# Attention ahead of a routed expert layer: the tokens' logits as products of their own, and one table for the order of the steps

## The chip, the core and the metric

The kernel runs on one core of a Trainium2 chip. The core has five engines with a queue each, which work through their instructions in program order and wait for each other through semaphores: TensorE (PE in the profile, with its weight loads as PEld), VectorE (DVE), ScalarE (ACT), GpSimd (POOL) and SyncE (SP), which here issues most of the DMA transfers. The metric is the device time of one execution in microseconds (us), lower is better. All data are 32-bit floats, unless something else is said.

## What is computed

The reference, cut to what matters:

```
B, H, S, Ns, D = 8, 8, 512, 32, 64            # attention
scores = x @ state.T * 0.125;  a = softmax(scores)     # tokens look at the 32 states
xread = a @ state                                      # a row for each token
scores2 = state @ x.T * 0.125; a2 = softmax(scores2)   # states look at the 512 tokens
sread = a2 @ x                                         # a row for each state
rows = concat(xread, sread) -> (8, 544, 512)           # heads side by side: 4352 rows of 512
...
logits = rows @ w_gate                                 # 8 experts
gate = sigmoid(rows @ w_local)
for each batch, for each row s in order:
    e = argmax(logits[s]) if s == 0 or gate[s] < 0.5 else the expert of the row before
    out[s] = softmax(logits[s])[e] * (relu(rows[s] @ w1[e]) @ w2[e])   # 512 -> 1024 -> 512
```

So every one of the 4352 rows goes through one of eight experts, and which one depends on the logits of that row and, through the gate, on the rows before it in its batch.

## The kernel before

The work has three stages, one after the other on TensorE.

**Attention** (classes `Attention` and `Batch`, lines 147 to 509). It goes batch by batch, b = 0 to 7. The eight heads of a batch lie as two groups (u = 0, 1) of four heads, 128 partitions each. For a batch:
- `scores` (L377): TensorE makes the scores of 128 head-and-state rows over 512 tokens, into two PSUM banks. Both softmaxes start from them.
- The softmax over states: `turned` (L410, VectorE transposes 32x32 blocks so that the 32 states lie along the free dimension), `over_states` (VectorE maximum L417, GpSimd subtraction L418), `exponents` (L422, ScalarE), `shares` (VectorE sum L426, L427, reciprocal L428, GpSimd product L429), `turn_back` (L435, VectorE transposes into the tile `a`).
- The softmax over tokens: `maximum` and `scaled` (L387, L391), `exponents_over_tokens` (L399, ScalarE, which also sums), `turn` (L445, transposes on TensorE), `turned_to` (L448, ScalarE copies them out), `state_reads` (L458, TensorE), `states_to` (L464, ScalarE), `states_to_rows` (L470 a transpose, L473 four DMAs to the tensor `rows` in DRAM).
- `token_reads` (L482): for each of four chunks c of 128 tokens, two products of `a` with the block-diagonal matrix `sd`. `sd` holds 256 state columns for each group and, beside them, the 9 columns of states times gate weights (`gates`, L212, L215), so that one product of 265 columns gives the values and a half of the token's nine logits. The 530 columns are copied to `xr` (L485), by VectorE for chunk 1 and by ScalarE for the others; GpSimd adds the two halves of the logits into `lt` (L507), and the values go to `rows` by one DMA for a batch (L508).
- `state_logits` (L500, L502): the logits of the 32 state rows.

The order of all these steps is written by hand in `run` (lines 224 to 355): three batches `now`, `then`, `later` are in work at once. Scores and transposes have one PSUM bank for each of four names (`s0`, `s1`, `t0`, `t1`), the values two tiles of two banks (`vps`). Every chunk of every batch is read before the stage ends.

**Routing** (class `Routing`). `choose` (L584 to L590) makes maxima and first-best experts from `lt`: once for batches 0 to 6, inside the attention, and once for batch 7 at the start of `route`. `route` then turns them to rows of 544 (`seq`, L611), carries the choice forward with a scan (L618, L620), turns back (`back`, L624), counts the rows of each expert (L637, L638), and works out, in a chain of small VectorE steps, in which slot each row is. `keep(n)` (L600) issues n products with no use for their result, 9 and 5 and 20 and 8 times. The expert of the first pair is known at L691; then SP issues its weights (L913), and after `two` (L763) GpSimd fetches the first 256 rows (L863).

**Experts** (`experts`, from L824). Rows are taken in pairs of blocks, 256 rows of one expert at a time, and nine small tiles. The first product is at L1139; from there TensorE works without a break. Its buffers are in memory that the attention has released.

Of the kernel before, what the change touches and what calls it, by code (L numbers as in the profile page):

```python
# [50 lines left out]
def kernel(  # L51
# [31 lines left out]
    def banks(ctx, n):  # L83
        ps = ctx.enter_context(tc.tile_pool(name="ps", bufs=n, space=PSUM))
        return lambda parts=P, n=512, dt=F32: ps.tile([parts, n], dt, tag="ps", name="ps")

# [6 lines left out]
    lt = keep.tile([P, B, NC, E + 1], F32, name="lt")  # L93

# [5 lines left out]
    with ExitStack() as phase:  # L100
        make_identity(nc, ident)
        start = Attention(phase, tc, xn, xt, st, stt, wgl, wgs, lt, rows)
        route.constants(ident)
        nc.gpsimd.memset(lt, 0.0)
        start.diagonal(range(2))
        nc.gpsimd.memset(none, 0.0)
        nc.sync.dma_start(out=rows[NT:].rearrange("o q x -> o (q x)"), in_=none)
        start.run(route)
    with ExitStack() as phase:
        bank = banks(phase, 6)  # L110

        sums = phase.enter_context(tc.tile_pool(name="sums", bufs=1, space=PSUM))
        sums = [sums.tile([P, 512], F32, name=f"sum{i}") for i in range(2)]
        experts(phase, tc, bank, sums, w1, w2, rows, slots, route, route.route(bank, sums, lt, slots), out)
# [21 lines left out]
A = G * SC * 4  # L136


class Attention:


    def __init__(self, ctx, tc, xn, xt, st, stt, wgl, wgs, lt, rows):
        nc = self.nc = tc.nc
        self.xn, self.xt, self.lt, self.rows = xn, xt, lt, rows
        self.wg, self.wh = wgs[:, 0], wgs[:, 1]
        once = ctx.enter_context(tc.tile_pool(name="once", bufs=1))
        self.xp = ctx.enter_context(tc.tile_pool(name="xp", bufs=3))
        self.wk = ctx.enter_context(tc.tile_pool(name="wk", bufs=2))
        self.tp = ctx.enter_context(tc.tile_pool(name="tp", bufs=2))
        self.sm = ctx.enter_context(tc.tile_pool(name="sm", bufs=4))  # L150
        self.ps = ctx.enter_context(tc.tile_pool(name="aps", bufs=1, space=PSUM))
        self.vps = ctx.enter_context(tc.tile_pool(name="vps", bufs=2, space=PSUM))

# [5 lines left out]
        self.x_t = {0: self.load_t(0)}  # L159
# [4 lines left out]
        self.x_t[1] = self.load_t(1)  # L164
        self.x_n = {0: self.load_n(0)}


        self.sd = once.tile([P, B, G * VW], F32, name="sd")
        nc.gpsimd.memset(self.sd, 0.0)
# [7 lines left out]
    def diagonal(self, ks):  # L177
        nc = self.nc
        for k in ks:
            r = slice(32 * k, 32 * k + 32)  # L180
            to = self.sd[r, :, E + 1:E + 1 + D].rearrange("p b (g d) -> p b g d", g=G)
            nc.scalar.copy(to[:, :, :, DH * k:DH * k + DH],
                           self.states_of[r].rearrange("p (b g d) -> p b g d", b=B, g=G))

    def load_t(self, b):
        nc = self.nc
        xs = []
        for i in range(2):
            x_t = self.xp.tile([P, KT // 2, S], F32, name=f"x_t{i}")
            nc.sync.dma_start(out=x_t.rearrange("p k s -> p (k s)"), in_=self.xt[b][:, i * D * 2:(i + 1) * D * 2])  # L190
            xs.append(x_t)
        return xs

    def load_n(self, b):
        x_n = self.xp.tile([P, SC, G, KT, DH], F32, name="x_n")
        self.nc.sync.dma_start(out=x_n.rearrange("p c u k d -> p (c u k d)"), in_=self.xn[b])
        return x_n
# [4 lines left out]
    def bank(self, name, parts=P):  # L202
        return self.ps.tile([parts, 512], F32, name=name)

    def gates(self):
        nc = self.nc
        ws = [self.bank(f"t{u}") for u in range(G)]
        for u, w in enumerate(ws):
            r = slice(64 * u, 64 * u + 64)
            for b in range(B):  # L210
                for k in range(KT):
                    nc.tensor.matmul(w[32 * k:32 * k + 32, b * (E + 1):(b + 1) * (E + 1)],  # L212
                                     lhsT=self.states(b)[r, k, :], rhs=self.wh[r, k, :], start=True, stop=True)
        for u, w in enumerate(ws):
            nc.scalar.copy(self.sd[:, :, u * (E + 1 + D):u * D + (u + 1) * (E + 1)],  # L215
                           w[:, :B * (E + 1)].rearrange("p (b e) -> p b e", b=B))

    def keep(self, n):

        for i in range(n):  # L220
            self.nc.tensor.matmul(self.idle[:, 0, :], lhsT=self.zero[:, :P], rhs=self.zero, start=True, stop=True)

    def run(self, route):

        self.ident = route.ident
        self.idle = self.vps.tile([P, G, 512], F32, name="v")
        self.keep(10)
        now, then = Batch(self, 0), Batch(self, 1)
        now.scores()
        for b in (2, 3):  # L230
            self.x_t[b], self.x_n[b - 1] = self.load_t(b), self.load_n(b - 1)

        for u in range(G):
            now.turned(u)
            now.over_states(u)
        now.maximum(0)
        now.scaled(0)
        now.exponents(0)
        self.gates()
        now.exponents(1)  # L240
        now.exponents_over_tokens(0)
        now.shares(0)
        now.maximum(1)
        now.scaled(1, self.nc.vector)
        now.exponents_over_tokens(1)
        now.shares(1)
        self.keep(6)
        now.turn(0)
        self.diagonal([2, 3])
        then.scores()  # L250
        now.turn(1)
        now.turn_back(0)
        now.turn_back(1)
        for u in range(G):
            then.turned(u)
            then.over_states(u)
        now.token_reads(0)
        now.turned_to(0)
        now.turned_to(1)
        now.state_reads()  # L260

        later = Batch(self, 2)
        self.load(0)
        then.maxima()
        then.exponents(0)
        then.exponents(1)
        then.exponents_over_tokens(0)
        then.shares(0)
        then.exponents_over_tokens(1)
        then.shares(1)  # L270
        now.invert()
        now.token_reads(1)
        now.states_to()
        now.token_reads(2)
        now.states_to_rows()
        later.scores()
        then.invert()
        later.maxima()
        then.turn(0)
        then.turned_to(0)  # L280
        then.turn(1)
        now.token_reads(3)
        then.turned_to(1)
        then.turn_back()
        later.exponents_over_tokens(0)
        later.turned(1)
        later.exponents_over_tokens(1)
        later.turned(0)
        later.over_states()
        now.logits()  # L290
        later.invert()
        then.token_reads(0)

        for b in range(1, B):
            now, then, later = then, later, Batch(self, b + 2) if b + 2 < B else None
            if later:
                later.scores()
            now.state_reads()
            self.load(b)
            if b == B - 2:  # L300
                then.turn(0)
                then.turn(1)
            if 1 < b < B - 1:
                now.turn_back()
            if b == B - 2:
                for u in range(G):
                    then.exponents(u)
                    then.shares(u)
                    if u == 0:
                        now.states_to()  # L310
            elif then:
                then.exponents()
                now.states_to()
                later.maxima()
            else:
                now.states_to()
            if b > 1:
                now.token_reads(0)
            if later:
                then.shares()  # L320
            now.token_reads(1)
            now.states_to_rows()
            if b == B - 2:
                then.turn_back(0)
            if later:
                then.turn(0)
                then.turn(1)
                later.exponents_over_tokens(0)
            if then:
                then.turned_to(0)  # L330
            now.token_reads(2)
            if then:
                then.turned_to(1)
            if b == B - 2:
                then.turn_back(1)
            if later:

                later.turned(1)
                later.exponents_over_tokens(1)
                later.turned(0)  # L340
                for u in range(G) if b == B - 3 else (None,):
                    later.over_states(u)
            if b == B - 1:
                route.choose(self.lt, 0, b)
                now.state_logits()
                now.token_reads(3)
# [923 lines left out]
```

## Time and profile before

| what | value |
|---|---|
| median of three runs | 560.93 us (559.71 to 562.62) |
| profiled execution, its own time | 559.81 us |
| its span, first to last instruction | 558.0 us |
| mean granted TensorE clock | 0.985 |
| TensorE busy over the span | 529.5 us, 95% |
| VectorE busy over the span | 377.8 us, 68% |
| TensorE's last token read of batch 7 ends (L482) | 83.30 us |
| first product of the experts starts (L1139) | 111.75 us |
| TensorE busy from 112 to 260, and from 260 to 400 us | 148.00 of 148, 140.00 of 140 |

How to read it: the span is cut by stage. In a stage, each engine's busy time is set against the stage's length, and then the timeline of one engine shows its instructions in order of start, each with the idle time ahead of it and what ended that idle time. Instructions overlap at their ends, so the time that one of a row of equal instructions costs is the distance from one start to the next, not its own duration. The row in the page that names the chain which ended last covers only the last instructions here, and says nothing of the attention.

### The profile page before, as it was taken

The page shows a single profiled execution, that of the slowest core. Times are in us where ns is not written, and L with a number is a line of the kernel's source. Part 1 is how long each engine was busy: PE and PEld are TensorE (multiplying, and loading weights), DVE is VectorE, ACT ScalarE, POOL GpSimd, SP SyncE. Part 2 cuts the span into 40 slices and gives each one's busy share as a digit, 9 for nine tenths or more (in the row PEclk, how much of TensorE's full clock was granted, in tenths as well). Part 3 has the DMA queues.
Part 4 walks back from the last instruction along what each step waited for, and adds up shares of the span by engine and source line. Part 5 has one row for each costly group of instructions (what it writes and reads, how often), then busy time and mean ns, then how long its engine had stood idle before and what let it go on. Part 6 is the DMA issues. An engine that isn't in the chain of part 4 may idle for free. (4 is left out here: it accounts for less than half of the span.)

```text
span 558.0 us, 12712 instructions
## 1 busy us (share of the span) xinstructions
PE 529.5 (95%) x4800; PEld 457.9 (82%) x4803; DVE 377.8 (68%) x625; ACT 168.1 (30%) x336; POOL 287.1 (51%) x366
## 2 busy tenths in 40 slices
PE   6879985999999999999999999999999999999994
PEld 2556662698989888898989898989899999989993
DVE  5879987673948474747565666665676766667674
ACT  4656651411132213231313122222232322223230
POOL 6444530165555555656464647463764546565454
PEclk9899997899999999999999999999999999999998
DMA  8999742689998989898979897966566575846652
GB/s 308 414 340 363 267 163 79 188 308 418 364 382 321 357 304 359 309 355 308 375 286 380 304 369 292 361 205 229 166 239 226 187 275 150 279 143 246 231 189 102
DMA packets 50793, 155.44 MB, mean 279 GB/s; under 512 B 9169, under 2 KB 9297, under 8 KB 47394
## 3 DMA queue, kind: packets, MB, share of 16 engines
q1 hardware_dynamic: 43202, 135.85, 66.6%
q0 software_dynamic: 7520, 18.69, 9.7%
q8 instruction: 40, 0.66, 0.5%
q14 instruction: 31, 0.25, 0.1%
HBM read 136.68 MB, written 17.89 MB: 277 GB/s over the span
## 5 line engine op out<-in xcount | busy, mean ns | idle before, releaser
L857 POOL DMA_INDIRECT xg<-rows,row x132 | 148.3, 1124 | 30.6 <-issue 30.1
L972 DVE TENSOR_TENSOR a<-a,a 128x1024 f32<-128x1024 f32 x64 | 76.8, 1220 | 21.1 <-DMA a<-in_w_dram 19.7
L1055 PE MATMUL ps<-xt,a 128*128 128x128 f32 x720 | 88.6, 276 | 0.0
L1055 PE MATMUL sum<-xs,a 128*128 128x128 f32 x720 | 87.8, 275 | 0.0
L1055 PEld LDWEIGHTS ps<-xt,a 128*128 128x128 f32 x720 | 84.4, 192 | 2.1 <-issue 1.8
L1055 PEld LDWEIGHTS sum<-xs,a 128*128 128x128 f32 x720 | 84.0, 192 | 0.0
L972 DVE TENSOR_TENSOR c<-c,c 128x1024 f32<-128x1024 f32 x64 | 75.4, 1219 | 3.0 <-DMA c<-in_w_dram 2.5
L1095 PE MATMUL ps<-c,h 128*128 128x256 f32 x312 | 74.7, 382 | 0.0
L1095 PEld LDWEIGHTS ps<-c,h 128*128 128x128 f32 x312 | 58.0, 190 | 10.9 <-issue 3.7
L1095 PE MATMUL ps<-c,hs 128*128 128x256 f32 x256 | 60.5, 379 | 0.0
L1038 POOL DMA_INDIRECT out_dram<-y,tok x32 | 34.5, 1079 | 43.6 <-DVE c L972 27.1
L1095 PEld LDWEIGHTS ps<-c,hs 128*128 128x128 f32 x256 | 48.6, 190 | 6.6
L1095 PE MATMUL sum<-c,h 128*128 128x256 f32 x200 | 47.2, 379 | 0.0
L972 DVE TENSOR_TENSOR h<-s,s 128x512 f32<-128x512 f32 x15 | 10.4, 692 | 54.2 <-ACT s L1078 54.2
L1095 PEld LDWEIGHTS sum<-c,h 128*128 128x128 f32 x200 | 38.0, 190 | 5.2
L871 POOL COPY tick<-s 1x1 f32<-1x1 f32 x45 | 16.3, 363 | 49.7 <-ACT s L1078 49.5
L482 PE MATMUL v<-sd,a 128*128 128x265 f32 x128 | 34.8, 406 | 4.7 <-DVE a L435 3.3
L1006 ACT COPY sum<-ps 128x256 f32<-128x256 f32 (+1 forms) x31 | 14.3, 460 | 71.0 <-PE ps L1055 49.5
L482 PEld LDWEIGHTS v<-sd,a 128*128 128x128 f32 x128 | 22.8, 193 | 12.0 <-DVE xr L485 3.5
L871 POOL COPY tick<-r 1x1 f32<-1x1 f32 x41 | 12.2, 299 | 36.6 <-ACT r L1100 34.3
L1100 ACT ACTIVATE r<-sum,prob 128x256 f32<-128x256 f32 x32 | 15.2, 475 | 51.7 <-PE sum L1095 49.2
L1095 PE MATMUL sum<-c,hs 128*128 128x256 f32 x128 | 30.2, 379 | 0.0
(228 smaller groups left out, 734.1 us busy)
## 6 DMA issues: line engine op xcount, KB each, us to landing
c<-in_w_dram SPq DMA_DIRECT2D x68, 512.0 KB, 7.8
a<-in_w_dram SPq DMA_DIRECT2D x64, 512.0 KB, 8.2
at<-in_w_dram SPq DMA_DIRECT2D x18, 1024.0 KB, 9.1
ct<-in_w_dram SPq DMA_DIRECT2D x18, 1024.0 KB, 7.8
x_t<-in_xt_dram SPq DMA_DIRECT2D x16, 512.0 KB, 7.9
x_n<-in_xn_dram SPq DMA_DIRECT2D x8, 1024.0 KB, 10.9
rows<-xr SPq DMA_DIRECT2D x8, 1024.0 KB, 4.2
xg<-rows,row POOLq DMA_INDIRECT x132, 5.2
```

The costliest lines, as they stand in the source:

```text
L482: nc.tensor.matmul(v[:, u, :VW], lhsT=self.a[:, u, c * P:c * P + P], rhs=at.sd[:, b, u * VW:(u + 1) * VW], start=True, stop=True)
L857: nc.gpsimd.indirect_dma_start(out=to.rearrange("p k t -> p (k t)"), out_offset=None, in_=rows.rearrange("n q x -> (n q) x"), in_offset=ba ...
L871: nc.gpsimd.tensor_copy(tick, value)
L972: nc.vector.tensor_tensor(out, a, b, op=op)
L1006: nc.scalar.copy(y, x)
L1038: nc.gpsimd.indirect_dma_start(out=out, out_offset=to, in_=y, in_offset=None, bounds_check=NT - 1, oob_is_err=False)
L1055: nc.tensor.matmul(to[:, m * P:m * P + P], lhsT=w[:, j, m * P:m * P + P], rhs=x[:, j, :], start=begin and m == 0 and j == 0, stop=(m == FK ...
L1095: nc.tensor.matmul(to, lhsT=x[:, m, :], rhs=w[:, m, :], start=begin and m == 0, stop=(m == FK // 2 - 1), skip_group_check=True)
L1100: nc.scalar.activation(to, t, Act.Copy, scale=p)
```

## The change

**The logits.** `sd` keeps only the 256 state columns of each group. The 9 columns of states times gates go to a tile of their own, `gl`, padded with zeros to 32 columns. A new step `logits` makes, for a batch, eight products of 32 by 128 outputs into one bank, over both groups, and `logits_turned` transposes that bank on VectorE into `lt`, which now has 32 columns for each chunk. GpSimd's addition of halves is gone.

**The values.** `token_reads` writes both groups, 512 columns, into one bank; all the copies to `xr` are ScalarE's.

**The order.** `run` and its three batches in work are gone. A string `STEPS` lists every step (two letters, batch, group or chunk), and `more` issues them in that order until a condition ends. Nearly all steps are now for one group (half a batch). The scores have four banks that rotate (`sp`), all else in the attention four banks (`p`); `e1` has five buffers of half a batch, `a` ten, `xr` three. In the table, `ch0` is `choose` for batches 0 to 6. All that stands after `ch1` is issued inside `route`: `reads(2)` and `reads(3)` take the places of `keep(9)` and `keep(5)`, a `reads(1)` follows `back`, and `reads(NB)` issues the rest after the counts. So eight of the 32 chunks (batch 5: one, batch 6: three, batch 7: four) are read inside the routing, with their ScalarE copies and the last three DMAs to `rows`. The third `keep` goes from 20 to 14. `route.more_constants` moves from the end of the attention to its start, and GpSimd's clearing of `gl`, `lt`, `sd` behind the constants.

**The memory.** What the late reads use (`a`, `xr`, `sd`, `lt`, bank pool `p`) is on the other side of memory and is released after the first yield of the routing; the experts' buffers are opened in two parts around this, and the routing has four banks until then, six after it.

The diff, cut to its core:

```
-        start.diagonal(range(2))
-        nc.gpsimd.memset(none, 0.0)
-        nc.sync.dma_start(out=rows[NT:].rearrange("o q x -> o (q x)"), in_=none)
+            start.clear()
+            route.more_constants()
             start.run(route)
...
+STEPS = """
+sc0 xt11 xt10 tr01 ga sd1 tr00 xt21 mx01 sd3 mo00 xt31 gl mo01 sb00 sd0 sc1 mx00 sb01 xn0 ex00 sd2 tr10 nb0 zs00
+et00 tr11 et01 xt20 tu00 mo10 ec00 iv0 tu01 sb10 mx10 xn1 ex01 mx11 ec01 zs01 ex10 nb1 sr0 zi01 et11 zs10 ml01
...
+tb60 vv53 ml71 xr42 tb70 lg6 wr4 xr53 tb71 vv60 lt6 ch0 lg7 xr60 vv51 vv52 lt7 xr51 ch1 vv73 xr52 vv70 xr73 vv50
+xr70 vv61 xr50 vv72 wr5 xr61 vv71 xr72 vv63 xr71 vv62 wr7 xr63 xr62 wr6
+"""
...
-        self.wk = ctx.enter_context(tc.tile_pool(name="wk", bufs=2))
+        self.wk = ctx.enter_context(tc.tile_pool(name="wk", bufs=5))
-        self.ps = ctx.enter_context(tc.tile_pool(name="aps", bufs=1, space=PSUM))
-        self.vps = ctx.enter_context(tc.tile_pool(name="vps", bufs=2, space=PSUM))
+        self.sp = ctx.enter_context(tc.tile_pool(name="sp", bufs=4, space=PSUM))
...
+    def clear(self):
+        nc.gpsimd.memset(self.gl, 0.0)
+        nc.gpsimd.memset(self.lt, 0.0)
+        nc.gpsimd.memset(self.sd, 0.0)
+        nc.gpsimd.memset(self.none, 0.0)
...
+        while self.steps and going():
+            name, at = self.steps.pop(0)
+            do[name](*at)
+    def reads(self, n):
+        def going():
+            nonlocal n
+            n -= self.steps[0][0] == "vv"
+            return n >= 0
+        self.more(going)
...
-        v = at.vps.tile([P, G, 512], F32, name="v")
-            nc.tensor.matmul(v[:, u, :VW], lhsT=self.a[:, u, c * P:c * P + P], rhs=at.sd[:, b, u * VW:(u + 1) * VW],
-                             start=True, stop=True)
-        copy = nc.vector.tensor_copy if c == 1 and b + 1 < B else nc.scalar.copy
-        copy(self.xr[:, c].rearrange("p (u d) -> p u d", u=G), v[:, :, :VW])
-        nc.gpsimd.tensor_tensor(at.lt[:, b, c, :], xr[:, c, :E + 1], xr[:, c, E + 1 + D:], op=Alu.add)
+    def logits(self, b):
+        l = self.of["l", b] = self.bank(n=P)
+        for u in range(G):
+            a = self.get("a", b, u).rearrange("p (i q t) -> p q i t", i=SC, q=Q)
+            for q in range(Q):
+                self.nc.tensor.matmul(l[SQ * q:SQ * q + SQ, :], lhsT=self.gl[:, b, u, :], rhs=a[:, q],
+                                      start=(u == 0), stop=(u == G - 1))
+    def logits_turned(self, b):
+        self.nc.vector.transpose(self.lt[:, b, :SC, :].rearrange("p i e -> p (i e)"), self.get("l", b))
+    def token_reads(self, b, c):
+        v = self.of["v", b, c] = self.bank()
+        for u in range(G):
+            d = slice(u * GD, u * GD + GD)
+            self.nc.tensor.matmul(v[:, d], lhsT=self.get("a", b, u)[:, c * P:c * P + P], rhs=self.sd[:, b, d],
+                                  start=True, stop=True)
+    def reads_kept(self, b, c):
+        xr = self.new(self.late, "xr", (b,), [P, SC, D], bufs=3)
+        self.nc.scalar.copy(xr[:, c], self.get("v", b, c))
...
-        keep(9)
+        reads(2)
         seq = bank(B, T, BF16)
...
-        keep(5)
+        reads(3)
         back = bank(P, NC * B, BF16)
...
+        reads(1)
         zp = rt.tile([P, COLS], F32, name="zp")
...
         nc.tensor.matmul(pre, lhsT=before, rhs=oh, start=True, stop=True)
+        reads(NB)
...
-        keep(20)
+        keep(14)
...
+    next(routing)
+    late.close()
+    bank.open(6)
```

The letters of the steps that are named below: `sc` scores, `tr` turned, `mx` maximum, `mo` over_states, `sb` its subtraction, `ex` exponents, `zs` sums, `zi` inverses, `ml` shares, `tb` turn_back, `et` exponents_over_tokens, `tu` and `ec` turn and turned_to, `iv` invert, `sr`, `st`, `rt`, `ws` the state reads, their scaling, transpose and DMAs, `sl` and `sk` the state logits, `lg` and `lt` the new logits and their transpose, `vv` and `xr` token_reads and their copies, `wr` the DMA of the values to `rows`, `xt` and `xn` the loads of x, `ga`, `gl`, `sd` the gate products, their copies and the diagonal copies.

## Prediction

> **What bounds the kernel now.** I read the page's slices first, then busy time by stretch, then the timelines of TensorE and VectorE. In the slices (13.95 us each):
>
> ```profile
> PE   6879985999999999999999999999999999999994
> DVE  5879987673948474747565666665676766667674
> PEclk9899997899999999999999999999999999999998
> ```
>
> TensorE is full from the eighth slice on, and short only in the first seven, the attention and the routing. The stretches (busy us of PE, PEld, DVE, ACT, POOL, then granted clock, DMA share, GB/s) say the same with numbers:
>
> ```profile
> 50.00:60.00 10.00, 9.48 (x126) 6.90 (x125) 9.33 (x18) 7.21 (x18) 4.25 (x4) 1.00 1.03 385
> 90.00:100.00 10.00, 5.78 (x19) 2.05 (x19) 8.72 (x37) 1.85 (x10) 0.00 (x0) 0.53 0.25 57
> 112.00:260.00 148.00, 148.00 (x1313) 133.03 (x1313) 94.72 (x145) 34.19 (x67) 84.44 (x106) 1.00 0.93 350
> ```
>
> In the attention TensorE and VectorE are both near 95%; in the routing VectorE works alone; behind 112 us TensorE has no gap, so whatever starts its first expert product (L1139) earlier ends the kernel earlier by as much. The diff leaves that stage's instructions alone. The prediction is thus the start of L1139, 111.75 us in the timeline of TensorE:
>
> ```profile
> 53.80 1.37 PE L377 MATMUL s<-x_t,sttc 64*32 64x512 f32 x16
> 55.10 1.10 PE L458 MATMUL t<-x_n,e 128*32 128x64 f32 x64
> 56.59 2.03 PE L482 MATMUL v<-sd,a 128*128 128x265 f32 x8 [0.39 <-DVE a L435]
> 58.45 1.04 PE L445 MATMUL t<-ident,e 128*128 128x128 f32 x8
> 59.33 2.36 PE L482 MATMUL v<-sd,a 128*128 128x265 f32 x8
> ...
> 84.39 2.12 PE L600 MATMUL sum<-place,identb 128*128 128x512 bf16 x8 [1.09 <-DVE lt L584]
> 86.44 0.39 PE L611 MATMUL ps<-identb,top 128*8 128x128 bf16 x4
> ...
> 88.77 0.25 PE L624 MATMUL ps<-identb,run 8*128 8x8 bf16 x4 [0.65 <-DVE run L620]
> ...
> 90.00 0.30 PE L637 MATMUL ps<-oh,ones 128*128 128x320 bf16 x1 [0.87 <-DVE oh L633]
> ...
> 111.75 13.44 PE L1139 MATMUL ps<-xt,a 128*128 128x128 f32 x118
> ```
>
> and of VectorE:
>
> ```profile
> 51.66 0.65 DVE L485 COPY xr<-v 128x530 f32<-128x530 f32 x1
> ...
> 53.74 1.22 DVE L417 TENSOR_REDUCE m<-e 128x32 f32<-128x1024 f32 x1
> ...
> 55.22 1.22 DVE L435 STREAM_TRANSPOSE a<-e 128x1024 f32<-128x1024 f32 x1
> 56.37 1.25 DVE L387 TENSOR_REDUCE nb<-s 128x1 f32<-128x512 f32 x2
> 58.08 1.22 DVE L426 TENSOR_REDUCE z<-e 128x32 f32<-128x1024 f32 x1 [0.47 <-ACT e L422]
> ...
> 76.52 1.26 DVE L435 STREAM_TRANSPOSE a<-e 128x512 f32<-128x512 f32 x2
> ```
>
> A batch takes 8.16 us (51.66 to the next such copy at 59.82); VectorE is idle for 0.47 of it, TensorE for 0.39. The last turn-back ends at 77.78; yet the routing's first transposes (L611) start at 86.44, since the reads of batches 6 and 7 come first and the logits come out of them.
>
> **What the Trainium skill says.** "TensorEngine Tiling (Array Packing)", Theoretical Speedup: up to 4x where one dimension is at most 32, as in the new logits. The trace agrees: 64 records of 64 columns with 32 output rows (L458) take about 1.1 us, 17 ns each, where 8 records of 265 columns at full width (L482) take 1.86 to 2.29, some 260 ns each: about four times less per column. "VectorE: DVE Perf Modes", the TRN2 errata section: a fixed cost per instruction. The trace agrees, but it is small from start to start: 0.60 us for a reduction of 512 (8.92 to 9.52), 1.14 for 1024, so 0.06 for a split. "TensorE: Matmul & The Clock Gate", Part 1: half clock after about 3.4 us idle, full again after as much work. Here the clock is 0.50 from 91 to 100 us, after TensorE fell idle at 90.4.
>
> **The parts, and their cost.**
>
> *TensorE, a batch.* Now 1.30 + 1.10 + 1.86 + 0.88 + 2.29 + 0.35 (L500) = 7.8 us. The reads narrow from 265 to 256 columns: 4.15 x 9/265, 0.14 less, about 1.0 a chunk. The logits add eight products, 16 records of 128 columns: 2048 columns against L458's 4096 in 1.1, so 0.55 (bounds: 0.3, and 2 if they don't overlap at all). New sum 8.2. Up to the last `lg7`, ten chunks (vv51, vv52 and the eight in the routing) are left behind it: 8 x 8.2 - 10 + 1.3 (gates) = 57 us from 5.9, so 63 plus waits. TensorE has slack for all but the worst bound.
>
> *VectorE, up to the last turn-back.* Before: 8.17 (first transpose) to 77.78 is 69.6, less waits of 5.25 (0.66, 0.55, 0.60, 1.59 and four of 0.46 or 0.47), so 64.4 of work. Removed: seven xr copies of 0.57, 4.0. Added: six transposes of logits, each like rt's L470 at 0.25, 1.5; some sixteen splits at 0.06, 1.0; inversion and rt of batch 7 come ahead of it, 0.5. Two pairs of inverses (L427, L428) fewer, 0.9. Sum 62.5. more_constants (1.9, 78.07 to 79.95) was behind 77.78 already; it goes to 3.6 to 5.5, where VectorE waits for the first scores, and is free as long as they don't come earlier.
>
> *Waits.* I followed the table with these durations. The one long wait is at the start: ex00 is behind three diagonal copies of 1.06 (L182) and the gates on ScalarE, so batch 0's token exponents end near 15.5 and iv0, with all of VectorE's queue behind it, waits some 2 us. After that the table puts work between each product and its use: five e1 buffers and a second batch of scores are ready ahead. I count waits of 2.3 in all (bounds 1 and, as before, 5.3). The turn-back ends at 8.17 + 62.5 + 2.3 = 73.0: **4.8 us earlier**.
>
> *Other queues.* ScalarE takes eight more copies of 0.5 to 0.6: from 6 to 6.4 us a batch, under VectorE's. GpSimd's clearing, 5.7 us (L169's 3.63 for 4240 columns, scaled to 5888, plus none's 0.66), runs from 1.8 to 7.5; the diagonals wait for data until 8.5 anyway. GpSimd loses seven additions of 0.26. SP: the loads are issued in the same order roughly; 16.8 MB of x must land by the turn-back, at 0.38 MB/us from 2 us that is 46 us, with 5 MB of writes 60. Hidden.
>
> *From the turn-back to the counts (L637).* Before: 77.78 to 86.44, 8.66. After, on VectorE: lt6 0.25, ch0 2.15 (80.09 to 82.24), lt7 0.25, ch1 1.17 (84.28 to 85.45), 3.8; on TensorE lg7's rest 0.6 and vv51, vv52, vv73, vv70 at 1.0, 4.7 with the hop. The later counts: 4.0 gained. Then 86.44 to 88.77 was 2.33; now seq's 0.5 and three reads of 1.0, 3.5, while the scan is done after 2.3: 1.2 lost. Back to counts was 1.23; now 0.35 and one read, 1.35: 0.1 lost. xr73 must wait for batch 4's write to land (its buffer), and the exponents (L616) are queued behind it; the write, 4.2 us to landing, has 2 us to spare before the sums (L627) are late. Net **2.5 us gained**. The last two reads lie in the 3.2 us that TensorE waits for `end` (L677). The last writes land some 3 us before the weights are fetched; gathers come 9 us later.
>
> *keep(14).* It ends nearly 2 us earlier than keep(20), which delayed the slot products (L757) by only 0.6, and their last part waits for VectorE at 103.5 anyway. Nothing, unless the clock is still half then: 4 us more for the 98-column products (3.88 now). The clock was full 5.7 us into keep(20); 14 last 5.2 to 6.
>
> Sum: 4.8 + 2.5 = 7.3. From the profiled execution's 559.81 this gives **552.5 us**. The median of the runs is 1.1 above that execution, inside their spread; I leave the number.
>
> **The rivals.**
>
> *VectorE waits as before or more.* For: VectorE's 123 steps stand in one fixed order, each with a hop between engines; the half clock of 20 to 22 us may come again. Against: the buffers. Waits of 6 instead of 2.3, and 0.5 lost in the tail: **556.7**.
>
> *No waits to speak of.* For: a transpose followed by its own reduction takes 0.75 (8.17 to 8.92), else 0.65, and the table separates most: 1.5 less work, 1 less waiting: **550.0**.
>
> *Nothing moves.* The DMAs set the pace: 25 MB at the 335 GB/s of 30 to 40 us take 75 us. Against: the writes of four batches may land after. **559**.
>
> *Slower: the clock.* TensorE at half clock in the attention. Price: one us more for each us of its work done so. It has 10 us of slack (63 against 73), and 7.3 of gain to lose: it decides from 17 us of work at half clock, two batches; at three batches, 24.6, the loss is 14.6 and the time **567**. For: TensorE's queue waits for another engine at nearly every step. Against: before it lasted 4 us in the attention, and gaps there stay under 1.7.
>
> **How the numbers follow.** Forecast 0.60, more waits 0.16, no waits 0.11, nothing moves 0.06, clock 0.07. Within 0.5% (2.8 us, about what measurements of this kernel can tell from no change) falls the third and a little of the first rival. Faster 0.86, same 0.07, slower 0.07. The range goes from 548.5 (no waits, and a tail without its losses) to 557.0 (the first rival); logits that don't overlap lie inside it.
>
> **What would show it.** Right: the first expert product near 104.5; the last turn-back near 73; no xr copy on VectorE; logits products about 0.55 a batch; VectorE over 95% from 16 to 73; TensorE's L611 4.7 behind the turn-back, the counts 5 after that. Wrong: a clock of 0.5 beyond 24 us; VectorE waiting for TensorE in mid-attention; L616 late; the expert stage longer than before.

## The result, and the profile after

The changed kernel takes 561.86 us (median of 19 runs, 559.08 to 564.96), the kernel before 559.77 (19 runs beside them): a ratio of 1.0036, 95% interval 1.0018 to 1.0053. So the change makes the kernel some 2 us slower, by less than the 0.5% within which the prediction called times the same; the forecast was 552.5. The profiled execution of the changed kernel took 562.38 us, with a span of 560.6 (before: 559.81 and 558.0), and a mean clock of 0.973 instead of 0.985.

The slices of the page, of the kernel after, 14 us each:

```profile
PE   6869898699999999999999999999999999999993
DVE  8977897583858484757565666665676666767673
PEclk9788899899999999999999999999999999999997
```

VectorE was to be over 95% busy in the attention. It isn't: the third and fourth slices are at 7, and the clock is at 7 or 8 in the second to fourth. From the ninth on TensorE is full as before. So most of the loss lies in the first eight slices, where the timeline of TensorE shows its longest idle time (start, duration, then in brackets the idle time and what ended it):

```profile
40.29 1.94 PE L377 MATMUL p<-x_n,e 128*32 128x64 f32 x64 [4.31 <-DMA x_n<-in_xn_dram]
41.97 1.11 PE L410 MATMUL p<-a,gl 128*32 128x128 f32 x16
43.00 4.14 PE L420 MATMUL p<-sd,a 128*128 128x256 f32 x12
```

TensorE stands 4.31 us for the load of x of batch 2 (`sr2`, the state reads) and then works slowly: 1.94 for 64 records that took 1.10 before, 1.11 for logits that take 0.64 elsewhere in the same trace. The stretches of that place (busy us of PE, PEld, DVE, ACT and POOL with counts, then clock, DMA share, GB/s) name the reason:

```profile
38.00:40.00 2.00, 0.00 (x0) 0.00 (x0) 0.69 (x1) 0.00 (x0) 1.05 (x1) 0.70 0.94 295
40.00:42.00 2.00, 1.71 (x65) 1.75 (x69) 0.00 (x0) 0.00 (x0) 0.00 (x0) 0.50 0.95 329
42.00:44.00 2.00, 2.00 (x28) 1.46 (x19) 0.87 (x3) 1.03 (x3) 0.00 (x0) 0.50 0.76 294
```

The clock is half from 38.8 to 45.6 us. From 40 to 42 neither VectorE, nor ScalarE, nor GpSimd does anything: all stand behind that one load, through the products of TensorE that come after it. VectorE's waits from its first transpose, at 9.20, to the last turn-back (in total, times, longest):

```profile
DVE lt L414 <- PE p L410: 4.6, 2, 4.4
DVE e L321 <- PE s L294: 1.7, 1, 1.7
DVE lt L402 <- PE p L398: 1.5, 1, 1.5
DVE rt L387 <- ACT ys L383: 1.1, 1, 1.1
DVE e L321 <- ACT e L310: 0.4, 1, 0.4
DVE a L358 <- POOL e L354: 0.3, 1, 0.3
```

They sum to 9.6; 2.3 were forecast. The two that follow the late load (4.4 at L414, 1.5 at L402) are 5.9 of them. The last turn-back, at 80.43 and 0.71 long, ends at 81.14 instead of 73.0 (77.78 before). Why the load came late is in SP's queue, which issues in order; first the issue of x of batch 2 in the kernel before, then the queue of the changed kernel:

```profile
12.19 0.33 SPq L196 DMA_DIRECT2D x_n<-in_xn_dram  x1
```

```profile
10.23 12.38 SPq L266 DMA_DIRECT2D x_t<-in_xt_dram  x4
22.71 3.45 SPq L393 DMA_DIRECT2D rows<-ys  x4
26.26 0.53 SPq L266 DMA_DIRECT2D x_t<-in_xt_dram  x1
26.93 2.46 SPq L393 DMA_DIRECT2D rows<-ys  x4
29.49 0.53 SPq L266 DMA_DIRECT2D x_t<-in_xt_dram  x1
30.06 2.00 SPq L270 DMA_DIRECT2D x_n<-in_xn_dram  x2
```

The last line holds `xn3` and then, at 31.6, `xn2`: the table has batch 2 behind batch 3. Both stand behind `ws0` and `ws1`, the eight writes of state rows, which take 3.45 and 2.46 us of SP, and behind four loads of `x_t` that keep SP from 10.23 to 22.61, since it waits there for earlier loads to land and for the scores that free their buffers. The transfer of `xn2` is done some 8.5 us after its issue; from 34 to 40 us the DMA engines are at a share of 0.94 to 1.03.

Behind the turn-back, in the timeline of TensorE:

```profile
85.79 0.39 PE L533 MATMUL ps<-identb,top 128*8 128x128 bf16 x4
...
89.01 0.25 PE L546 MATMUL ps<-identb,run 8*128 8x8 bf16 x4
...
90.27 0.30 PE L560 MATMUL ps<-oh,ones 128*128 128x320 bf16 x1
...
95.42 3.19 PE L523 MATMUL ps<-place,identb 128*128 128x512 bf16 x14
102.03 0.42 PE L681 MATMUL ps<-bf,inp 128*128 128x4 bf16 x8 [3.42 <-DVE inp L675]
...
104.33 3.22 PE L523 MATMUL sum<-place,identb 128*128 128x512 bf16 x8
...
113.39 1.83 PE L1069 MATMUL ps<-xt,a 128*128 128x128 f32 x14
```

From the turn-back to the counts (L560) it is now 9.13 us, 12.22 before. From the counts to the first product of the experts it is 23.12, 21.75 before. The balance at that product: turn-back 3.4 later, the tail 3.1 shorter, the rest 1.4 longer, so 113.39 - 111.75 = 1.64 us late. What remains of the span's 2.6 lies in the expert stage (447.2 us to the end, 446.25 before), which I don't explain: in the kernels below, whose expert stage is the same, it ran from 445.9 to 450.0.

### The profile page after: what moved, and what is told of

It is laid out like the page before. It is cut to its first block, busy times and chain, and to the rows that moved or that the text cites. A ratio compares the mean times of both kernels' runs of the same rounds, so it can differ in the third digit from the quotient of the medians.

```text
span 560.6 us, 12943 instructions
## 1 busy us (share of the span) xinstructions
PE 529.4 (94%) x4905; PEld 462.3 (82%) x4905; DVE 380.2 (68%) x635; ACT 172.5 (31%) x348; POOL 288.1 (51%) x369
## 5 line engine op out<-in xcount | busy, mean ns | idle before, releaser
L787 POOL DMA_INDIRECT xg<-rows,row x132 | 151.0, 1144 | 30.6 <-issue 29.6
L801 POOL COPY tick<-s 1x1 f32<-1x1 f32 x45 | 13.6, 303 | 47.2 <-ACT s L1008 47.1
L420 PE MATMUL p<-sd,a 128*128 128x256 f32 x128 | 33.0, 402 | 0.1
L985 PE MATMUL ps<-xs,a 128*128 128x128 f32 x240 | 29.3, 275 | 0.0
```

The lines of the kernel that those rows point to most:

```text
L420: self.nc.tensor.matmul(v[:, d], lhsT=self.get("a", b, u)[:, c * P:c * P + P], rhs=self.sd[:, b, d], start=True, stop=True)
L787: nc.gpsimd.indirect_dma_start(out=to.rearrange("p k t -> p (k t)"), out_offset=None, in_=rows.rearrange("n q x -> (n q) x"), in_offset=ba ...
L801: nc.gpsimd.tensor_copy(tick, value)
L985: nc.tensor.matmul(to[:, m * P:m * P + P], lhsT=w[:, j, m * P:m * P + P], rhs=x[:, j, :], start=begin and m == 0 and j == 0, stop=(m == FK ...
```

## The experiments

All edits are to the changed kernel. Ratios are to the kernel before, run beside each on the same chip; different chips give that kernel 559.4 to 561.2 us, so only ratios are compared, and 0.001 is 0.56 us. Each kernel has one trace. The attention has the same instructions in the changed kernel, `e2_keep28` and `e4_reads_early`, and its last turn-back ends at 81.14, 79.56 and 81.32 us; likewise in `e1_xn2` and `e5_xn2_keep28`, at 77.14 and 75.79. So a difference of less than 2 us there, between two traces, shows nothing of an edit.

The theory: one load in the wrong place of SP's queue costs the attention its gain, the half clock behind the wait is part of the price, and `keep(14)` loses some more. Its rivals: the new order itself has the waits, or the late reads don't pay, or VectorE's slow casts at the start push everything back.

**The load alone** (`e1_xn2`), `xn2` right behind `xn1`; the two table lines of the diff:

```
-et00 tr11 et01 xt20 tu00 mo10 ec00 iv0 tu01 sb10 mx10 xn1 ex01 mx11 ec01 zs01 ex10 nb1 sr0 zi01 et11 zs10 ml01
+et00 tr11 et01 xt20 tu00 mo10 ec00 iv0 tu01 sb10 mx10 xn1 xn2 ex01 mx11 ec01 zs01 ex10 nb1 sr0 zi01 et11 zs10 ml01
...
-xr01 mx20 xn3 sl1 xr03 tb11 vv02 nb2 et21 mo20 lg1 zs21 et20 sb20 tu21 lt1 mo30 ec21 xn2 sc4 iv2 sb30 ex20 sk1
+xr01 mx20 xn3 sl1 xr03 tb11 vv02 nb2 et21 mo20 lg1 zs21 et20 sb20 tu21 lt1 mo30 ec21 sc4 iv2 sb30 ex20 sk1
```

> Batch 2's x_n (xn2) is issued right behind xn1, ahead of the DMAs that wait for state reads. Theory (a late place in SP's queue): TensorE's wait of 4.31 us at the state reads of batch 2 and the half clock behind it go; the last turn-back ends 5 to 7 us before the changed kernel's 81.14, and the time is 4 to 7 us below the changed kernel. Rival (the DMA engines set the pace): the same bytes come, so another load is late instead; the turn-back stays within 2 us of 81, the time within 2 us.

Measured: 557.44 us, ratio 0.996 (0.9945 to 0.9975), 0.76% or 4.2 us under the changed kernel. The same step in its timeline of TensorE, and the last turn-back in VectorE's:

```profile
36.41 1.10 PE L377 MATMUL p<-x_n,e 128*32 128x64 f32 x64
```

```profile
76.43 0.71 DVE L358 STREAM_TRANSPOSE a<-e 128x512 f32<-128x512 f32 x1 [0.30 <-POOL e L354]
```

No wait, full speed, and the turn-back ends at 77.14, 4.0 earlier; first expert product 109.70 (3.7 earlier). So the place of this one load is the main cause, and it alone decides whether the change is faster than before. It isn't all: the turn-back gained less than the 5 to 7 expected, and VectorE's waits up to it still sum to 5.7. TensorE now waits 0.92 for x of another batch at 59.18, and has half clock from 58 to 65.

**The clock alone** (`e3_fill`): 72 products without a use fill the wait ahead of `sr2`, in the bank that it is about to write.

```
+        for i in range(72 if b == 2 else 0):
+            self.nc.tensor.matmul(r.rearrange("p u d -> p (u d)"), lhsT=self.zero[:, :P], rhs=self.zero[:, :P], start=True, stop=True)
```

> 72 products of 128 columns with no use are put ahead of batch 2's state reads, where TensorE waits 4.31 us for data. Theory: the wait itself is the main loss and stays; only the half clock from 39 to 45 us goes, 2 to 2.5 us of the time. Rival (the clock is the main loss): 4 us or more. If the fillers outlast the wait, it is up to 1 us worse.

Measured: 559.93 us, ratio 1.0011 (0.9994 to 1.0028). The load still lands as late, but the work behind it runs at full clock:

```profile
40.12 1.10 PE L379 MATMUL p<-x_n,e 128*32 128x64 f32 x64 [0.38 <-DMA x_n<-in_xn_dram]
...
46.65 1.09 PE L294 MATMUL s<-x_t,sttc 64*32 64x512 f32 x16
```

These next scores start at 49.34 in the changed kernel and at 43.46 in `e1_xn2`. So up to there the late load costs 5.9 us, of which 2.7 are the half clock and 3.2 the wait itself. Further on the gain can't be told: TensorE waits 1.42 for another x at 62.38, the turn-back ends at 79.21, which `e2_keep28` comes near (79.56) without such an edit, and the time's interval overlaps that of the changed kernel.

**More for the clock in the routing** (`e2_keep28`).

```
-        keep(14)
+        keep(28)
```

> keep(14) becomes keep(28). Theory (TensorE idles 3.4 us behind keep(14), falls to half clock and does the eight following fillers slowly): these take about 1.7 us instead of 3.22, the first expert product starts 1.5 us sooner after the counts, the time is 1.5 us below the changed kernel. Rival (28 fillers delay the slot products, or the clock is not what holds them): nothing or some tenths later.

Measured: 560.28 us, ratio 1.0021 (1.0008 to 1.0034). Its timeline of TensorE:

```profile
93.85 7.71 PE L523 MATMUL ps<-place,identb 128*128 128x512 bf16 x28
101.39 1.50 PE L681 MATMUL ps<-bf,inp 128*128 128x4 bf16 x40
102.76 1.89 PE L523 MATMUL sum<-place,identb 128*128 128x512 bf16 x8
```

The 3.42 us of idle time are gone, and eight products take 1.89 instead of 3.22. From the counts (88.68) to the first expert product (110.52) it is 21.84 us, 1.3 less. The whole time doesn't show this apart from the changed kernel, since the intervals overlap. The traces show it in four of the five kernels with 28 products, with 21.80 to 21.84 us; the fifth, `e10_fill_too`, takes 23.26 (see the last section). The six with 14 take 22.46 to 23.44.

**Late reads undone** (`e4_reads_early`): all chunks are read ahead of the routing's first transposes, and useless products stand in for them again.

```
-tb60 vv53 ml71 xr42 tb70 lg6 wr4 xr53 tb71 vv60 lt6 ch0 lg7 xr60 vv51 vv52 lt7 xr51 ch1 vv73 xr52 vv70 xr73 vv50
-xr70 vv61 xr50 vv72 wr5 xr61 vv71 xr72 vv63 xr71 vv62 wr7 xr63 xr62 wr6
+tb60 vv53 ml71 xr42 tb70 lg6 wr4 xr53 tb71 vv60 lt6 ch0 lg7 xr60 vv51 vv52 lt7 xr51 vv73 xr52 vv70 xr73 vv50
+xr70 vv61 xr50 vv72 wr5 xr61 vv71 xr72 vv63 xr71 vv62 wr7 xr63 xr62 wr6 ch1
...
-        reads(2)
+        keep(9)
...
-        reads(3)
+        keep(5)
```

> All 32 chunks are read ahead of the last choice, keep(9) and keep(5) are back; the rest is the changed kernel. Theory (reading eight chunks inside the routing gained what the steps predicted): the first transposes of the routing come 4 to 6 us later behind the turn-back, the scan's end to the transposes back is 1.2 us shorter, the time is 2.5 to 4.5 us above the changed kernel. Rival (late reads only move work that TensorE must do anyway): the same time within 1 us.

Measured: 567.79 us, ratio 1.0152 (1.0126 to 1.0178), 6.5 us above the changed kernel; the counts come at 96.65 instead of 90.27. In the timelines of TensorE and VectorE:

```profile
82.31 8.90 PE L420 MATMUL p<-sd,a 128*128 128x256 f32 x40
91.05 2.11 PE L523 MATMUL ps<-place,identb 128*128 128x512 bf16 x9
93.09 0.39 PE L533 MATMUL ps<-identb,top 128*8 128x128 bf16 x4
```

```profile
93.63 0.43 DVE L540 TENSOR_SCALAR hold<-ps 8x544 bf16<-8x544 bf16 x1 [8.17 <-PE ps L534]
```

Ten chunks in one row keep TensorE until 91.05, while VectorE waits 8.17 us for the transposed logits. So reading late does pay, more than the 2.5 to 4.5 expected: this table leaves ten chunks behind the last turn-back, and would be worse than the old order without it.

**The casts** (`e7_casts`): GpSimd copies one element that needs the casts' results ahead of its clearing, so that the clearing starts behind them.

```
-            start.clear()
+            start.clear(route.raw[4])
...
+        nc.gpsimd.tensor_copy(self.none[:, :1], identb[0:1, 0:1])
         nc.gpsimd.memset(self.gl, 0.0)
```

> GpSimd starts its clearing only after VectorE's three casts (one small copy of a cast's result stands ahead of it). Theory (the casts of 5.3 us are slow because GpSimd clears at the same time, and cost nothing in the end, since batch 1's scores come later anyway): the casts take under 1 us each, the last turn-back moves by less than 1 us, the time stays within 1 us of the changed kernel. Rival (the late start of the first transposes goes through to the end): 1 us or more earlier.

Measured: 563.09 us, ratio 1.0041 (1.0022 to 1.0059), as the changed kernel. In VectorE's timeline, of the changed kernel and then of this one:

```profile
1.54 5.35 DVE L452 CAST iof<-io 128x128 f32<-128x128 int32 x1 [0.40 <-POOL io L445]
1.68 5.27 DVE L454 CAST iob<-io 128x128 bf16<-128x128 int32 x1
```

```profile
1.54 0.33 DVE L453 CAST iof<-io 128x128 f32<-128x128 int32 x1 [0.40 <-POOL io L446]
1.68 0.25 DVE L455 CAST iob<-io 128x128 bf16<-128x128 int32 x1
...
2.16 5.22 DVE L471 TENSOR_SCALAR before<-iob,part 128x128 bf16<-128x128 bf16 x1
```

The stall isn't gone, it has moved to the next instruction of the kind. The first transpose starts at 8.65 instead of 9.20, and the gain is lost at once: VectorE then waits 2.16 for the second scores (1.68 before the edit). What the other half of the late start costs was not tested.

**The clock at the start** (`e8_fill_start`): six useless products of 512 columns ahead of batch 1's scores (`sc1`).

```
+        for i in range(6 if b == 1 else 0):
+            self.nc.tensor.matmul(s[0], lhsT=self.zero[:, :P], rhs=self.zero, start=True, stop=True)
```

> Six fillers with no use ahead of batch 1's scores in the changed kernel, where TensorE waits for x; the kernel before had six fillers (keep(6)) near this place, the changed one has none. Theory (the half clock from 11 to 22 us is a lesser loss): the clock there is full earlier, batch 1's scores take 1.1 instead of 1.96, but the wait for xn2 takes up what is gained, so the time is within 1 us of the changed kernel. Rival (the slow start is a main cause): 2 us or more below it.

Measured: 563.29 us, ratio 1.004 (1.0021 to 1.0059), as the changed kernel. VectorE's first wait falls from 1.68 to 0.67 us. The late load takes it back: in this kernel's timeline of TensorE

```profile
40.16 1.93 PE L379 MATMUL p<-x_n,e 128*32 128x64 f32 x64 [4.37 <-DMA x_n<-in_xn_dram]
```

against 40.29 in the changed kernel. With `xn2` in its old place this product starts at 40.07, 40.12, 40.43, 39.74 and 40.16 us in `e2_keep28`, `e3_fill`, `e4_reads_early`, `e7_casts` and `e8_fill_start`, whatever was done ahead of it: the load sets the time, and nothing earlier counts.

**Load and fillers together** (`e5_xn2_keep28`): the edits of `e1_xn2` and `e2_keep28`.

> xn2 early and keep(28) together. Theory (two separate losses that add): the first expert product starts about 1.3 us before the one of the kernel with xn2 early alone (109.70), the time is 1 to 2 us below that kernel's 557.44. Rival (the clock behind keep(14) differs from run to run and the filler changes nothing on the mean): within 0.5 us of it.

Measured: 557.21 us, ratio 0.9936 (0.9913 to 0.9959); turn-back 75.79, counts 84.91, first expert product 106.71. That is 3.0 us ahead of `e1_xn2`, where 1.3 was expected: 1.6 come behind the counts, where the edit is, and 1.35 from an attention with the same instructions, which is chance. The time's interval overlaps that of `e1_xn2`. Left on VectorE are waits of 4.5 us in all.

**One more load ahead** (`e6_all`): `e5_xn2_keep28`, the fillers of `e8_fill_start`, `sl4` seven places later, and x of batch 5 earlier. The loads and writes in SP's order:

```
-xn4 xt71 xt70 wr1 wr2 xn5
+xn4 xn5 xt71 xt70 wr1 wr2
```

> xn2 early and keep(28), and three more places of the table: xn5 ahead of the two writes to rows, sl4 behind tu71, and six fillers ahead of batch 1's scores. Theory (what is left of the attention's loss is waits of TensorE and the half clock that each brings): the last turn-back comes at 72 to 75, the first expert product at 104 to 107, the time is 552.5 to 555.5. Rival (VectorE's work fills the stage once the long wait is gone): the turn-back stays within 1 us of 77, the time at 556.

Measured: 559.02 us, ratio 0.9961 (0.9946 to 0.9977): a miss, with the turn-back at 77.94 where 72 to 75 was expected and `e5_xn2_keep28` had 75.79 (the intervals of the two times overlap). Its timeline of TensorE shows the next load in line late:

```profile
54.32 1.96 PE L295 MATMUL s<-x_t,sttc 64*32 64x512 f32 x16 [3.67 <-DMA x_t<-in_xt_dram]
```

From 40 to 50 us its DMA engines are at a share of 0.97, from 50 to 56 at 0.98. With no bandwidth to spare, a load put ahead makes another one late. `e10_fill_too` below differs from this kernel, in SP's order, in the place of that load alone (behind `xt71` and `xt70`): there the same scores start at 50.55 without a wait, and the ratio is 0.9911, with an interval that doesn't meet this one.

**Writes behind, not loads ahead** (`e9_writes_late`): `e5_xn2_keep28` with `sl4` seven places later, and in SP's order

```
-xn4 xt71 xt70 wr1 wr2 xn5
+xn4 xt71 xt70 xn5 wr1 wr2
```

> xn2 early and keep(28), and the writes of batches 1 and 2 to rows (wr1, wr2, 1 MB each, needed by nobody in this stage) are issued behind the load xn5 instead of ahead of it; sl4 stands behind tu71. Theory (transfers are taken in the order of SP's queue while the DMA engines are full, so a write ahead of a load delays it): batch 5's state reads (1.19 us) no longer wait for x, the scores of batch 7 still do by about 1 us; the last turn-back is at 74 to 75.5 instead of 75.8 and the time 0.5 to 2 us below that of xn2 with keep(28) alone, as a ratio to the kernel before 0.990 to 0.993. Rival (the wait moves to another load, as when xn5 went ahead of the x_t of batch 7): ratio 0.9936 or above.

Measured: 557.7 us, ratio 0.9928 (0.9907 to 0.995); turn-back 76.81, a miss (74 to 75.5 was expected). The wait for x at `sr5` is gone. In its place TensorE stands 1.62 and 2.00 us in the middle of two batches' state reads, from 53.4 and 59.5, which the profile puts down to no other engine and no transfer; that stays open. The time can't be told from that of `e5_xn2_keep28`.

**With the fillers at the start** (`e10_fill_too`): `e9_writes_late` and the six products of `e8_fill_start`.

> The same with six fillers ahead of batch 1's scores. Theory (without the long wait behind it, an earlier full clock at the start is worth something): batch 1's first transposes wait 0.6 instead of 1.5 us, the turn-back is 0.5 to 1 us earlier, the ratio 0.001 to 0.002 lower. Rival (the loads set the pace between 10 and 60 us): the same ratio within 0.001.

Measured: 556.09 us, ratio 0.9911 (0.9884 to 0.9939), the best here, some 5 us under the kernel before; its interval overlaps those of `e5_xn2_keep28` and `e9_writes_late`, not that of `e1_xn2`. VectorE's waits from 9 us to the last turn-back:

```profile
DVE lt L415 <- PE p L411: 0.8, 1, 0.8
DVE rt L388 <- ACT ys L384: 0.6, 1, 0.6
DVE e L322 <- PE s L295: 0.5, 1, 0.5
DVE e L322 <- ACT e L311: 0.4, 1, 0.4
DVE a L359 <- POOL e L355: 0.3, 1, 0.3
DVE z L316 <- ACT e L311: 0.2, 1, 0.2
```

They sum to 2.8 (5.3 in `e9_writes_late`), and the turn-back ends at 75.16. The first wait for scores is 0.5 instead of 1.2. So with the late load away the fillers seem to keep what they gain, but one trace of each doesn't settle it; and the first expert product starts at 107.54, hardly ahead of `e9_writes_late` (107.76), since the clock falls behind the counts.

## Why the prediction was wrong

**The step that failed** is "SP: the loads are issued in the same order roughly; [...] Hidden." I compared bytes with bandwidth (46 us for x, 60 with the writes) and didn't follow SP's queue step by step, though I did so for VectorE. The order was not the same: x of batch 2 went from 12.19 to 31.6 us, behind batch 3's, behind writes, and behind loads that wait for buffers. The term that it spoiled is "waits of 2.3": 9.6 measured. With work as forecast (81.14 - 9.20 - 9.6 = 62.3, where 62.5 stood) the turn-back comes at 81.14. `e1_xn2` puts the load back in its place and gets 4.0 back, half of the 8.1 by which the turn-back missed; the waits that it leaves, 5.7, were still put too low.

**The start.** 9.20, where I kept 8.17. That the clearing "runs from 1.8 to 7.5; the diagonals wait for data until 8.5 anyway" looked at who needs the cleared tiles, not at whom the clearing stops. The Trainium skill, "SBUF — State Buffer", section "SBUF: two separate sides", says that GpSimd and some of VectorE's instructions (its two-port modes, and some with two inputs) share a pair of ports as an exclusive lock: whichever starts first has it, the other blocks. The trace fits: the casts end at 6.89 and 6.95, when the clearing of `sd` ends (3.30 + 3.50 = 6.80), and in `e7_casts`, where the clearing starts behind them, they take 0.33 and 0.25. Whether the casts run in such a mode the trace doesn't say. In that kernel 0.55 of the 1.0 us came back, and the time didn't change.

**The mechanism held, once the loads were in place.** In `e10_fill_too` the waits are 2.8 and the sum is 9.2 + 63.2 + 2.8 = 75.2, so 2.2 above the forecast: 1.0 of start, 0.5 of waits, 0.7 of work. That is a kernel with five more edits, and at 0.9911 it is still short of the ratio that was forecast (552.5 / 559.81 = 0.987).

**The tail.** L533 4.65 behind the turn-back (forecast 4.7), back 3.2 later (3.5), counts 1.26 after that (1.35): net 3.1 gained where 2.5 stood (the prediction's own terms, 4.0 - 1.2 - 0.1, give 2.7). Right, and a little low. Logits at 0.57 to 0.64 us a batch (forecast 0.55) were right too.

**keep(14)**, "Nothing, unless the clock is still half then [...] 14 last 5.2 to 6", missed by 1.4 us. The danger was named, but with the wrong size of the filler: 14 products take 5.95 in `e4_reads_early`, where TensorE is cold, but 3.19 here, because the late reads had kept it warm. So TensorE fell idle for 3.42 us ahead of the slot products and was at half clock from 103.65 to 107.07.

**When the clock falls.** I took the 3.4 us of the Trainium skill's "TensorE: Matmul & The Clock Gate", Part 1, for a length of idle time that a gap must reach. The page speaks of windows of that length which run freely and don't start anew with the kernel. The traces agree with the windows: in the changed kernel up to 110 us the granted clock changes at 4.67, 11.49, 21.73, 38.80, 45.63, 62.69, 66.11, 103.65 and 107.07 us, and every distance is a whole multiple of 3.41. So the clock fell at 38.80, when TensorE had been idle for only 2.8 us (since 35.98); in the kernel before it fell at 90.57, 0.14 us after TensorE fell idle, behind small products with gaps of 0.65 and 0.87. And it fell at 62.69, behind a wait of only 1.79:

```profile
62.19 0.42 PE L398 MATMUL p<-wgs,rt 128*32 128x9 f32 x8 [1.79 <-DVE z L349]
62.54 1.87 PE L364 MATMUL p<-ident,e 128*128 128x128 f32 x8
64.34 1.92 PE L377 MATMUL p<-x_n,e 128*32 128x64 f32 x64
```

There the same 64 records as in `e1_xn2` above take 1.92 instead of 1.10, so gaps "under 1.7" were less of a reassurance than I took them for. In `e2_keep28`, with the same instructions up to there, this wait is 1.30, the clock stays full, and the turn-back ends 1.6 us earlier. Where the windows lie relative to the work differs from trace to trace (in `e1_xn2` the clock falls at 58.10, which is no whole number of 3.41 us from 62.69), so which gap is punished is in part chance. How much of a window must be busy no run here settles.

**The rivals.** "VectorE waits as before or more" had the right term, VectorE's waits, and put 6 for 9.6. "The clock" was there in part: by stretch, about 5.5 us of TensorE's work at half clock from 10 to 20 us, 2 from 20 to 30, 5 from 38 to 46 and 3 from 62 to 66 (its busy time, by the part of the stretch that the mean clock puts at half), some 15 against the 17 from which I let it decide. Its price of one us for each was too simple: `e3_fill` returns 2.7 at the next scores for the 5 or so at 40 us, and less at the turn-back, `e8_fill_start` nothing. "The DMAs set the pace" was true of one place, around 40 us, by order, and of another from 50 to 64 us: by bandwidth in `e6_all`, and with waits for x of 0.92 to 1.53 us in `e1_xn2`, `e3_fill`, `e5_xn2_keep28`, `e7_casts` and `e8_fill_start`. It was not true of the whole stage.

**What stays open.** The up to 4 us by which the expert stage differs between kernels with the same instructions in it; how much of `e10_fill_too` over `e5_xn2_keep28` is real, since the times don't separate them; and the idle time within the state reads of `e9_writes_late`.

## What to carry to other kernels

When an order is rewritten, follow every in-order queue through it, SP's too: for each load, find what stands ahead of it and when that can be issued; a check of bytes against bandwidth says nothing of one late transfer, and where the DMA engines are full, moving one load ahead delays another. Filler products are sized for the clock and the gap of the place where they stand: count the gap again when the work ahead of them changes. Compare two traces of the same instructions before a difference of one or two us is put down to an edit. And a gain ahead of a fixed arrival is no gain: mend the last late thing first, then the small ones show.

## What was not expected of the hardware

VectorE's casts of 128x128 took 5.3 us beside GpSimd's clearing and 0.25 to 0.33 free of it, and they waited through three clearings in a row (from 1.73 to 6.80), not for one of them. Half clock also followed thin work: in `e10_fill_too` the clock is half from 98.59 to 102.01, behind 2.5 us of products of 4 columns with no gap over 0.40,

```profile
96.06 0.43 PE L682 MATMUL ps<-bf,inp 128*128 128x4 bf16 x8 [0.40 <-DVE inp L676]
...
98.58 3.16 PE L524 MATMUL sum<-place,identb 128*128 128x512 bf16 x7
```

where seven such products took 1.67 in `e5_xn2_keep28`. That is the 1.4 us that its 28 fillers were to save. `e9_writes_late`, with the same instructions from the turn-back on, stays at full clock there and saves it, so the same fillers save it in one trace and not in another.
